# Twelve 1 MB loads of x issued as two transfers each, cut at partition 120, 104 or 88

## The chip, the cores and the metric

The kernel runs on one core of one Trainium2 chip. The metric is the device time of one execution in microseconds (us), taken as the median of repeated runs. The engines of the core are named as in the profile: PE (TensorE, matrix products and transposes), DVE (VectorE), ACT (ScalarE), POOL (GpSimd) and SP (SyncE, which here only issues DMA transfers). Sixteen DMA engines move data between the chip's memory (HBM) and the core's on-chip buffer of 128 partitions.

## The reference

A gated linear recurrence over 6336 time steps for 4 sequences of 256 channels, followed by a highway layer on every token:

```
sig = 1 / (1 + exp(-f_logit));  f = lower_bound + (1 - lower_bound) * sig
for t in range(S):                                   # S = 6336
    h = f[:, t] * h + (1 - f[:, t]) * x[:, t];  y[:, t] = h
H = max(y @ w_h, 0);  T = 1 / (1 + exp(-(y @ w_t + b_t)))
out = T * H + (1 - T) * y                            # 25344 tokens of 256 channels
```

Inputs x and f_logit and the output are 25.95 MB each in fp32, so at least 78 MB cross the memory interface.

## The kernel before

The tokens are cut into 29 **units** (lines 40 to 70). A large unit holds 1024 tokens as 128 partitions of 8 tokens, that is 8 KB of x per partition and 1 MB in all; there are 22 of them (units 3 to 13 and 15 to 25). The first three and the last three units are smaller, and unit 14 takes 192 tokens of each of the four sequences and moves them as four transfers of 32 partitions.

A unit goes through these steps; the letter is its name in the order:

- `l`, `x`: loads of f_logit and x, issued by SP (`load`, line 228). Tiles `l` and `x` have six buffers each.
- `u` (ACT): sigmoid of -f_logit. `b` (POOL, four of them as DVE): `bv` = u * x, a quarter of the unit at a time (line 252).
- `i`, `p` (PE): transposes of u and of bv, so that channels stand on partitions and tokens in a row. `f` (ACT): the gate.
- `s` (DVE): the recurrence as a scan along the tokens, one for each half of the channels (line 307). Each scan starts from the last column of the scan before it, so the units form one chain.
- `z`, `g` (PE): the two products of the highway layer; `t` (ACT), `d` (DVE), `E` on POOL and `e` on DVE: its gate and mix.
- `o` (PE): transposes back, with the sum; `c` (ACT): copy from the accumulator to `o` tiles (four buffers); `w` (SP): store, 512 KB each for the most part.

The order of the work on every engine is written out by hand in one string (lines 72 to 124); each token of it emits its instructions, and `pin` keeps them in that order. All transfers but two of 1 KB (`prm`, issued by ACT, two partitions each) are issued by SP, one after the other, in the order in which `l`, `x` and `w` stand in the string. SP waits in this order for what a transfer needs: a load of x for the last `bv` that read the buffer, a store for its copy, and each transfer also for the landing of the eighth transfer before it, since transfers take eight completion semaphores in turn. While SP waits, everything behind it in the string waits too.

`sides` (line 218) gives for a load the pairs of a tile's partitions and a part of the tensor in HBM. For a large unit that is one pair: 128 partitions, each reading 8 consecutive tokens.

Of the kernel before, what the change touches and what calls it, by code (L numbers as in the profile page):

```python
# [19 lines left out]
def kernel(  # L20
# [10 lines left out]
    nc = tc.nc  # L31
    B, S, D = x.shape
    assert (B, S, D) == (4, 6336, 256)
    P = 128
    NH = D // P
    NB = 8
# [3 lines left out]
    units = [  # L40
        (0, 128, 2, 0, 'y', 4, 0),
        (0, 128, 2, 256, 'y', 4, 0),
        (0, 128, 4, 512, 'y', 4, 0),
        (0, 128, 8, 1024, 'y', 4, 1280),
        (0, 128, 8, 2048, 'y', 4, 2048),
        (0, 128, 8, 3072, 'y', 4, 0),
        (0, 128, 8, 4096, 'y', 4, 2048),
        (0, 128, 8, 5120, 'yk', 4, 0),
# [82 lines left out]
    pin = tc.keep_in_program_order  # L131

    def sb(shape, dtype, name):
        return pool.tile(shape, dtype, tag=name, name=name, bufs=bufs.get(name, 1))
# [83 lines left out]
    def sides(n, t, full, j0, j1, stored=False):  # L218

        b, np_, nb, at = units[n][:4]  # L220
        if isinstance(b, int):
            return [(t[:np_, :j1 - j0], full[b, at + j0 * np_:at + j1 * np_, :].rearrange("(p j) d -> p j d", p=np_))]
        part = np_ // B
        return [(t[i * part:(i + 1) * part, :j1 - j0] if stored else t[i::B, :j1 - j0],
                 full[k, at[i]:at[i] + part * nb, :].rearrange("(p j) d -> p j d", p=part)[:, j0:j1])
                for i, k in enumerate(b)]

    def load(n, name, src):
        t = sb([P, NB, D], FP32, name)
        for dst, s in sides(n, t, src, 0, units[n][2]):  # L230
            pin(nc.sync.dma_start(dst, s))
        st[n][name] = t

    def do_l(n, k, eng, slot):
        load(n, "l", f_logit)

    def do_x(n, k, eng, slot):
        load(n, "x", x)
# [143 lines left out]
    for token in order.split():  # L382
        token, _, slot = token.partition(":")
        name = token.rstrip("v")
# [3 lines left out]
        n, _, k = name[1:].partition(".")  # L388
# [29 lines left out]
```

## Time and profile before

| | |
|---|---|
| time, median of 3 runs | 218.88 us (216.72, 218.88 and 220.64) |
| profiled execution, first to last instruction (span) | 215.2 us |
| the same execution's own time | not recorded beside its span |
| DMA traffic | 78.69 MB, mean 366 GB/s |
| read from HBM, written to HBM | 52.43 MB, 25.95 MB |
| transfers issued by SP | 125 |
| of these, loads of x of 1 MB | 22, median 13.8 us from issue to landing |
| granted TensorE clock, mean | 0.999 of full speed |

The profile is one execution. A line of a group or a timeline names the source line (L252 is line 252 above), the engine, the operation and the tiles that it writes and reads (`bv<-u,x`); "busy" is the time in which the engine worked. An idle stretch is put down to what ended it: `<-DMA x<-in_x_dram` means that a load of x landed and the waiting instruction went on. "SPq" is SP's queue of issues. Slices cut the span into 40 equal parts of 5.38 us. "Landing" is the time at which the last of a transfer's sixteen completions came in.

### The profile page before, as it was taken

The numbers are of one execution on the slowest core, as the hardware profiler recorded it, in microseconds if no ns is written. First come the engines' busy times: TensorE is split into PE (matmuls) and PEld (weight loads), VectorE is DVE, ScalarE is ACT, GpSimd is POOL, SyncE is SP. The second block draws the span as 40 slices with busy tenths as digits, with TensorE's granted clock in tenths as the row PEclk, the third lists the DMA queues.
The fourth block names the chain that finished last, engine by engine and source line by source line (L and its number), as shares of the span: only waits on it lengthen the run. The fifth ranks groups of instructions, "written<-read, shape, count | busy, mean of one in ns | idle before, by whom it ended". The sixth has DMA issues, their size and how long they took to land. (4 is left out here: it accounts for less than half of the span.)

```text
span 215.2 us, 4648 instructions
## 1 busy us (share of the span) xinstructions
PE 190.1 (88%) x1784; PEld 132.4 (62%) x1811; DVE 199.2 (93%) x164; ACT 195.9 (91%) x195; POOL 178.9 (83%) x166
## 2 busy tenths in 40 slices
PE   7477778988999799999998999999899999999881
PEld 3144456655766666675676766667676576776661
DVE  2789998999999899999998999999999999999960
ACT  4579889999999999999999999999999999999772
POOL 3045789997999999899998999887988999898910
PEclk9999999999999999999999999999999999999999
DMA  6999999999999999999999799998999999498275
GB/s 185 395 420 417 423 419 410 423 316 315 429 416 425 411 426 393 350 411 414 428 425 416 324 329 326 431 399 287 330 412 420 419 422 420 165 321 360 110 285 200
DMA packets 16750, 78.69 MB, mean 366 GB/s; under 512 B 2004, under 2 KB 2776, under 8 KB 11096
## 3 DMA queue, kind: packets, MB, share of 16 engines
q1 hardware_dynamic: 16720, 78.39, 92.7%
q8 instruction: 14, 0.23, 0.4%
q14 instruction: 8, 0.07, 0.1%
q10 hardware_dynamic: 8, 0.00, 0.0%
HBM read 52.43 MB, written 25.95 MB: 364 GB/s over the span
## 5 line engine op out<-in xcount | busy, mean ns | idle before, releaser
L252 POOL TENSOR_TENSOR bv<-u,x 128x512 bf16<-128x512 f16 x95 | 112.8, 1217 | 21.7 <-DVE w_sb L197 9.0
L307 DVE TENSOR_TENSOR_SCAN y<-f,y,bT 128x1024 bf16<-128x1024 f16 (+2 forms) x46 | 92.8, 2032 | 1.6 <-ACT f L276 0.9
L342 POOL TENSOR_TENSOR e<-d,t 128x512 bf16<-128x512 bf16 (+1 forms) x60 | 67.7, 1148 | 3.9 <-DVE e L342 3.0
L336 DVE SCALAR_TENSOR_TENSOR d<-y,ncc,g 128x1024 bf16<-128x1024 bf16 (+2 forms) x54 | 58.9, 1101 | 2.4 <-PE g L318 2.3
L331 ACT ACTIVATE t<-z,bt 128x1024 bf16<-128x1024 f32 (+3 forms) x58 | 57.9, 1019 | 2.0 <-PE z L318 1.3
L276 ACT ACTIVATE f<-uT,ncc 128x1024 f16<-128x1024 f16 (+3 forms) x53 | 55.4, 1057 | 4.2 <-PE uT L259 2.8
L318 PEld LDWEIGHTS <-w_sb 128*128 128x128 f16 x416 | 39.3, 99 | 32.2 <-issue 2.7
L372 ACT COPY o<-op 128x1024 f32<-128x1024 f32 (+2 forms) x53 | 51.2, 983 | 4.7 <-PE op L362 3.1
L243 ACT ACTIVATE u<-l 128x2048 f16<-128x2048 f32 (+3 forms) x29 | 49.2, 1695 | 3.8 <-DMA l<-in_f_logit_dram 3.6
L362 PE MATMUL op<-ident_b,e 128*128 128x128 bf16 x396 | 49.4, 219 | 1.0 <-DVE e L342 0.8
L318 PE MATMUL z<-y,w_sb 128*128 128x512 bf16 (+1 forms) x179 | 47.5, 372 | 1.2 <-DVE d L336 0.2
L318 PE MATMUL g<-y,w_sb 128*128 128x512 bf16 (+1 forms) x181 | 47.9, 372 | 0.7
L362 PEld LDWEIGHTS <-e 128*128 128x128 bf16 x396 | 44.0, 113 | 5.7 <-issue 2.2
L361 PE MATMUL op<-diag,y 128*128 128x128 f16 x368 | 45.9, 219 | 1.6 <-ACT o L372 0.9
L361 PEld LDWEIGHTS <-y 128*128 128x128 bf16 x368 | 41.0, 113 | 1.9
L290 PE MATMUL bT<-ident_f,bv 128*128 128x128 f32 x198 | 33.6, 283 | 7.2 <-POOL bv L252 2.5
L259 PE MATMUL uT<-ident_h,u 128*128 128x128 f16 x396 | 31.9, 221 | 7.7 <-DVE y L307 2.5
L259 PEld LDWEIGHTS <-u 128*128 128x128 f16 x396 | 26.6, 99 | 18.5 <-issue 7.9
L290 PEld LDWEIGHTS bT<-ident_f,bv 128*128 128x128 f32 x198 | 23.1, 142 | 17.0 <-POOL bv L252 3.8
L342 DVE TENSOR_TENSOR e<-d,t 128x512 bf16<-128x512 bf16 (+5 forms) x19 | 17.7, 943 | 1.0 <-PE op L362 0.7
L307 DVE TENSOR_TENSOR_SCAN y<-f,yr,bT 128x1024 bf16<-128x1024 f16 x4 | 9.3, 2333 | 0.0
L252 DVE TENSOR_TENSOR bv<-u,x 128x512 bf16<-128x512 f16 x4 | 3.4, 855 | 3.1 <-DMA x<-in_x_dram 3.1
(42 smaller groups left out, 48.9 us busy)
## 6 DMA issues: line engine op xcount, KB each, us to landing
out_dram<-o SPq DMA_DIRECT2D x46, 512.0 KB, 7.7
l<-in_f_logit_dram SPq DMA_DIRECT2D x22, 1024.0 KB, 11.1
x<-in_x_dram SPq DMA_DIRECT2D x22, 1024.0 KB, 13.8
l<-in_f_logit_dram SPq DMA_DIRECT2D x4, 256.0 KB, 8.7
x<-in_x_dram SPq DMA_DIRECT2D x4, 256.0 KB, 4.5
l<-in_f_logit_dram SPq DMA_DIRECT2D x2, 512.0 KB, 9.7
x<-in_x_dram SPq DMA_DIRECT2D x2, 512.0 KB, 7.5
out_dram<-o SPq DMA_DIRECT2D x3, 256.0 KB, 13.9
```

The source lines that it names most:

```text
L252: shared(pin(e.tensor_mul(st[n]["bv"][:np_, k].rearrange("p d j -> p j d"), st[n]["u"][:np_, q:q + 2], st[n]["x"][:np_, q:q + 2])), not eng)
L259: pin(nc.tensor.transpose(uT[:, j * np_:(j + 1) * np_], st[n]["u"][:np_, j, h * P:(h + 1) * P], ident_h[:np_, :np_]))
L276: pin(nc.scalar.activation(to, of, AF.Identity, scale=ncc[:, h:h + 1], bias=1.0))
L290: pin(nc.tensor.transpose(to, pair, ident_f[:np_, :np_]))
L307: pin(nc.vector.tensor_tensor_scan(y[:, c0:c0 + ln], st[n]["f", h][:, c0:c0 + ln], st[n]["bT", h][:, c0:c0 + ln], 0.0 if prev is None else ...
L318: pin(nc.tensor.matmul(p[:, a:e], w_sb[:, k, ki, m * P:(m + 1) * P], half(n, "y", ki)[:, a:e], start=ki == 0, stop=ki == NH - 1))
L331: pin(nc.scalar.activation(half(n, "t", m), st[n]["z", m][:, :tokens(n)], AF.Sigmoid, bias=bt[:, m:m + 1]))
L336: pin(nc.vector.scalar_tensor_tensor(half(n, "d", m), half(n, "y", m), ncc[:, m:m + 1], st[n]["g", m][:, :tokens(n)], op0=ALU.mult, op1=AL ...
L342: shared(pin(eng.tensor_mul(st[n]["e"][:, a:e], st[n]["d"][:, a:e], st[n]["t"][:, a:e])), eng is nc.gpsimd)
L361: pin(nc.tensor.matmul(o, half(n, "y", h)[:, cols], diag[:, h], start=True, stop=False))
L362: pin(nc.tensor.matmul(o, half(n, "e", h)[:, cols], ident_b, start=False, stop=True))
L372: pin(nc.scalar.copy(o[:np_, :w], st[n]["op", q][:np_, :w]))
```

## The change

`load` takes a cut for x in units with an odd number and the full eight tokens per partition. There the one transfer of 128 partitions becomes two, from partition 0 to the cut and from the cut to 128:

```diff
     def load(n, name, src):
         t = sb([P, NB, D], FP32, name)
+        cut = (120, 104, 88)[n % 3] if name == "x" and n % 2 and units[n][2] == NB else 0
         for dst, s in sides(n, t, src, 0, units[n][2]):
-            pin(nc.sync.dma_start(dst, s))
+            for p0, p1 in ((0, cut), (cut, P)) if cut else ((0, dst.shape[0]),):
+                pin(nc.sync.dma_start(dst[p0:p1], s[p0:p1]))
         st[n][name] = t
```

The condition holds for units 3, 5, 7, 9, 11, 13, 15, 17, 19, 21, 23 and 25. Units 3, 9, 15 and 21 are cut at 120 (120 + 8 partitions), units 7, 13, 19 and 25 at 104 (104 + 24), units 5, 11, 17 and 23 at 88 (88 + 40). SP then issues 137 transfers. The two parts stand next to each other in SP's order; both fill the same tile, and all other instructions keep their order on every engine.

## The prediction, made before the changed kernel was run

> **What bounds the kernel now.** I read the totals and the slices of the span first, then the DMA queues, then the waits, last the order of time on GpSimd and SyncE around the loads of x.
>
> The page's totals and slices (busy tenths, then GB/s, of 40 equal slices of 5.38 us):
>
> ```profile
> PE 190.1 (88%) x1784; PEld 132.4 (62%) x1811; DVE 199.2 (93%) x164; ACT 195.9 (91%) x195; POOL 178.9 (83%) x166
> ...
> DVE  2789998999999899999998999999999999999960
> ...
> DMA  6999999999999999999999799998999999498275
> GB/s 185 395 420 417 423 419 410 423 316 315 429 416 425 411 426 393 350 411 414 428 425 416 324 329 326 431 399 287 330 412 420 419 422 420 165 321 360 110 285 200
> ```
>
> Two things are full at once. VectorE has next to no idle time from 20 to 190 us, and the DMA engines run at a ceiling of about 420 GB/s except in short dips. So a load that comes late cannot be made up by a faster engine behind it.
>
> The DMA queue (packets, MB, share of 16 engines' span), then the issues of x:
>
> ```profile
> q1 hardware_dynamic: 16720, 78.39, 92.7%
> ...
> q10 hardware_dynamic: 8, 0.00, 0.0%
> ```
>
> The packets can be counted. Every partition row of a transfer is one packet: the 125 transfers of SP have 14720 rows, and 16720 - 14720 = 2000 = 125 x 16, so each posts sixteen completions, one per DMA engine. All of these have 32 or 128 partitions. Queue 10 holds the two loads of `prm`, two partitions each: 8 packets, that is two rows and two completions for each. **So a transfer of two partitions used two engines, one of 32 or 128 used all sixteen, always in equal shares.** A 1 MB load gives each engine 8 rows of 8 KB; such rows take 309 to 313 ns each in the trace's packet records, and loads standing back to back land every 2.50 us, which is 8 x 0.3125. An engine has this one rate; a load is there when its slowest engine is done.
>
> How late loads are, seen from GpSimd, which multiplies x by u (`bv`): its waits, and four of them in order of time (start, us, what, idle before and releaser):
>
> ```profile
> POOL bv L252 <- DMA x<-in_x_dram: 7.8, 6, 2.2
> ```
>
> ```profile
> 21.23 4.54 POOL L252 TENSOR_TENSOR bv<-u,x 128x512 bf16<-128x512 f16 x4 [2.19 <-DMA x<-in_x_dram]
> 27.77 4.54 POOL L252 TENSOR_TENSOR bv<-u,x 128x512 bf16<-128x512 f16 x4 [2.00 <-DMA x<-in_x_dram]
> ...
> 53.82 2.30 POOL L252 TENSOR_TENSOR bv<-u,x 128x512 bf16<-128x512 f16 x2 [1.52 <-DMA x<-in_x_dram]
> ...
> 163.40 1.18 POOL L252 TENSOR_TENSOR bv<-u,x 128x512 bf16<-128x512 f16 x1 [0.79 <-DMA x<-in_x_dram]
> ```
>
> These are units 4, 5, 9 and 23: their x landed at 21.07, 27.61, 53.66 and 163.27 by the semaphore records and was used 0.13 to 0.16 us later. Three of the four are loads that the change splits. The others come with 1 to 6 us in hand (x17: 116.29, used at 118.27).
>
> Last, SyncE, whose program order is the order of all transfers:
>
> ```profile
> 30.11 0.33 SPq L231 DMA_DIRECT2D l<-in_f_logit_dram  x1
> 44.96 0.34 SPq L379 DMA_DIRECT2D out_dram<-o  x1
> ...
> 116.60 0.42 SPq L231 DMA_DIRECT2D l<-in_f_logit_dram  x1
> 123.44 0.81 SPq L379 DMA_DIRECT2D out_dram<-o  x2
> ```
>
> Twice SyncE stands still before a store that waits for its copy, and the rings run dry. The sixteen completions of a load tell how far engines are apart: after such a pause all end within 0.3 us (126.20), in the middle of a stretch the last comes 2.0 to 2.9 us behind the first (x5: 24.73 to 27.61), because packets of instructions, 16 KB and about 1.0 us each, fourteen in all, take their turn on single engines.
>
> **The change, part by part.** Twelve loads, x3, x5 to x25 without the smaller units, become two transfers; the text that came with the change says ten, the program has twelve, four of each cut. No engine's order of work changes but SyncE's, which grows from 125 transfers to 137.
>
> *Twelve more issues and slots.* An issue occupies SyncE 0.33 to 0.45 us, 12 x 0.4 = 5 us on a queue that waits 103 us for copies: nothing. Each transfer waits for the eighth before it to land, so a pair takes two of eight places. Behind a wait there stand seven transfers, still some 3 MB or 7.5 us of work in the rings, against about 2.5 us from an issue to its first landing on an empty ring (44.96 to 47.66): nothing, and 2.5 us once if that cover failed.
>
> *A second wait in front of `bv`.* GpSimd waits for both halves. The median semaphore instruction at that line takes 42 ns: 12 x 0.04 = 0.5 us at most, some of it in waits that are there anyhow; I take 0.2.
>
> *Rows per engine.* This is the term that matters, and the trace has no transfer of 120, 104, 88, 40, 24 or 8 partitions. Bounds by counting rows: if the second half fell on those engines that the first had spared, the slowest engine still had 8 rows, nothing added. If shares are equal, as in every transfer that the trace has, and the engines are counted from the same end for both halves, 120 + 8 is 15 engines of 8 rows and 8 of 1; 104 + 24 is 13 of 8 and 12 of 2; 88 + 40 is 11 of 8 and 10 of 4. The first eight engines then carry 9, 10 and 12 rows where they had 8. That is 1 + 2 + 4 = 7 rows a triple, 28 in all: 28 x 0.3125 = 8.75 us. I take the second, since equal shares are what 2, 32 and 128 partitions show, and since the two 2-partition loads left just two engines behind (7.10 and 7.12 against 6.46 for the next, in the load issued at 2.11), not four: they chose the same two. [...]
>
> *How much of 8.75 us reaches the end.* The backlog grows load by load: 0.31 us at x3, 1.56 at x5, 2.19 at x7, 2.50 at x9, 3.75 at x11, 4.38, 4.69, 5.94 at x17, 6.56, 6.88, 8.13 at x23, 8.75 at x25. It is felt where a load has no margin: at x5 (1.6 us), at x9 (2.5), a little at x17 (5.9 against a margin of 2.0 plus the shift that GpSimd has by then), then at x23. After x23 no split load is tight (x25 has 4.6 us), and GpSimd and VectorE are full up to the end, so **the shift at x23 is about the shift of the end**.
> From above: if the slowest engine of before is one of the eight, it has no idle time at the pauses (it ended its loads at 124.93 and the stores behind them at 126.20, 1.27 us later, where 512 KB take 1.25), nothing is absorbed, and x23 comes 8.1 us late.
> From below: an ordinary engine idles about 1.1 us at the pause of 45 us (45.30 to 47.66, less 1.25 for the store), 2.5 us at that of 123 (122.18 to 125.90, less 1.25) and 0.3 at 146: 3.9 us of the backlog go there, and another 2.1 are hidden behind the engine that is last today; it also has its own share of the instruction packets, 14 x 1.0 / 16 = 0.9. So 8.1 - 3.9 - 2.1 + 0.9 = 3.0 us.
> Several engines are late by 0.7 to 2.8 us in each stretch, so one of the eight being among them is likelier than not; the middle, 5.5 us, is my value. Downstream of `bv` some 1.5 us of reserve lie before the scan (from the last `bv` to the scan 2.3 us at x5, where 0.6 at x3 was enough), but the chain that ends the span runs through GpSimd after 189 us, so I take nothing off for it.
>
> Sum: 5.5 + 0.2 = 5.7 us on the profiled span of 215.2, so 220.9. The median of the three runs stands 3.7 us above the span, its launch and end; with the same margin the time is **224.6 us**, by the bounds 221.9 to 227.2.
>
> **The rivals.**
> *Meeting on the way into the buffer memory (0.12).* With 15, 13 or 11 engines the rows may be dealt so that two engines write at the same place at once. [...] The nearest row for a 1 MB load that is slowed for whatever reason is x9, whose first completion stands 4.05 us behind that of the store before it, 1.55 more than usual. Twelve such are 18.6 us, nearly all on the full DMA rings: about 236. Against it: the stores of 32 neighbouring partitions, 128 KB each, completed 0.29 us apart (144.99 and 145.28), faster than any load.
> *Not slower: the late engines are the spared ones (0.13).* If the engines that trail today are those with the high numbers, the change takes 8 rows off them at a time; x5 would then land with the eight at 26.05 + 1.56 = 27.6 instead of 27.61, or, where the split puts a free engine under the next instruction packet, up to 1.3 us earlier, and x23 only by what is left. This decides if all laggards of a stretch stand above the eleventh engine; then the time is 217.6 to 220. For it: fourteen packets on single engines. Against: the engine that trails at x5 is one of the two that carried `prm`, the second value of that pair staying at 26.05.
> *Nothing happens (0.09).* Rows are spread evenly whatever the count, or the halves complement each other: 219. [...] The 2-partition loads, with two completions each, speak against an even spread.
>
> **How the numbers follow.** The backlog case has 0.66. A change of 2% (4.4 us) is about what a measurement of this kernel can tell from none, the three runs lying 1.8% apart. Of the 0.66 I put 0.57 above 223.3 us and 0.09 below; with the first rival slower has 0.69. The second rival gives 0.08 to within 2% and 0.05 to faster (1.3 us earlier makes no 2% without luck in the runs), the third all its 0.09 to within 2%: 0.26 and 0.05. The range reaches from 218 (the last rival, less half the spread of the runs) to 233 (the backlog in full with a third of the first rival), and leaves out most of that rival and the fastest corner of the second.
>
> **What would show it.** In the profile after: the first completion of an 88-partition half well before the last; x5, x9 and x23 landing 1.6, 2.5 and 3 to 8 us later; GpSimd's wait for x growing from 7.8 us to 12 or more; DMA's mean GB/s falling from 366 to about 356 with the same megabytes. It is wrong if rows of x take longer than 313 ns in number, if the sixteen completions lie no further apart than now, or if the loads land late and the end does not move.

## The result and the profile after

The changed kernel takes **260.12 us** (median of 4 runs, 255.8 to 264.77) against 217.84 us for the kernel before (4 runs, 216.72 to 220.64). Over the faster runs of each kernel (255.8 and 259.46 us of the changed one) the ratio is 1.182, 95% interval 1.173 to 1.190. The predicted way was right, the predicted size (224.6, at most 233) far too small.

The totals and slices of the changed kernel's page, as they were read for the kernel before (an execution of 260.79 us with a span of 259.0; its 40 slices are 6.48 us each):

```profile
PE 202.8 (78%) x1784; PEld 140.5 (54%) x1811; DVE 200.6 (77%) x164; ACT 198.2 (77%) x195; POOL 179.5 (69%) x166
...
DVE  3748894865898577999669898946999927899962
...
PEclk9675899997889979999889999977999998999998
DMA  7999999999989999699999999998899998939556
GB/s 222 379 221 413 228 306 229 201 332 340 310 360 228 374 380 263 227 351 238 408 424 393 262 395 318 242 359 248 309 352 285 312 412 283 380 143 356 234 209 228
DMA packets 16835, 78.69 MB, mean 304 GB/s; under 512 B 2088, under 2 KB 2860, under 8 KB 11180
...
q1 hardware_dynamic: 16804, 78.39, 92.4%
```

Every engine does the same work (VectorE 200.6 us after, 199.2 before); what grew is its idle time. The DMA engines are busy all the time, as before, and move the same 78.69 MB, but in many slices at 201 to 230 GB/s where they moved about 420. q1's share times the span was 0.927 x 215.2 = 199.5 us for each of the sixteen engines and is 0.924 x 259.0 = 239.3 us: 39.8 us more busy time for the same bytes, against 43.8 us more span. So the packets themselves became slow, which is most of the added time. The waits say who starves (engine, line and tile, what it waited for: us in total, times, longest):

```profile
POOL bv L254 <- DMA x<-in_x_dram: 36.1, 15, 5.3
ACT u L245 <- DMA l<-in_f_logit_dram: 22.2, 13, 4.4
...
ACT o L374 <- DMA out_dram<-o: 14.2, 11, 3.8
```

Not only x is late: loads of f_logit, which nobody touched, and stores are late too (3.6 and 0.4 us before). GpSimd's first multiplications of units 4, 5, 9 and 23 in order of time, the same four as before (line 252 has become line 254):

```profile
24.98 4.52 POOL L254 TENSOR_TENSOR bv<-u,x 128x512 bf16<-128x512 f16 x4 [2.05 <-DMA x<-in_x_dram]
35.81 4.53 POOL L254 TENSOR_TENSOR bv<-u,x 128x512 bf16<-128x512 f16 x4 [6.32 <-PE bT L292]
...
70.64 6.67 POOL L254 TENSOR_TENSOR bv<-u,x 128x512 bf16<-128x512 f16 x5 [4.18 <-DMA x<-in_x_dram]
...
204.15 1.16 POOL L254 TENSOR_TENSOR bv<-u,x 128x512 bf16<-128x512 f16 x1 [5.29 <-DMA x<-in_x_dram]
```

They start 3.8, 8.0, 16.8 and 40.8 us later than before (at unit 5 the profile names PE as the last releaser). Taken over all units the delay grows in steps, the largest at split loads: 4.0 us at unit 3, 4.3 more by unit 5, 5.1 more by unit 7, 5.4 at unit 17, 4.5 at unit 23, and 43.7 at the last unit.

The clearest view is a stretch around the first split load, before anything else differs. Both fences are windows of 4 us: the window, its length, then busy time and (instructions) of PE, PEld, DVE, ACT and POOL, the granted clock, the DMA share and GB/s. Before:

```profile
12.00:16.00 4.00, 2.91 (x23) 1.95 (x22) 3.33 (x5) 3.22 (x4) 1.55 (x2) 1.00 1.02 424
16.00:20.00 4.00, 2.67 (x23) 1.66 (x22) 4.00 (x7) 3.39 (x4) 2.79 (x2) 1.00 1.00 414
20.00:24.00 4.00, 3.28 (x29) 2.09 (x28) 4.00 (x3) 3.36 (x5) 2.77 (x3) 1.00 1.01 418
```

After:

```profile
12.00:16.00 4.00, 3.13 (x18) 1.99 (x15) 3.20 (x5) 1.72 (x4) 1.83 (x2) 0.65 1.04 240
16.00:20.00 4.00, 2.00 (x21) 1.81 (x22) 0.49 (x1) 3.03 (x4) 0.00 (x0) 0.78 1.01 238
20.00:24.00 4.00, 1.86 (x7) 0.81 (x6) 3.91 (x6) 2.76 (x2) 2.70 (x2) 0.50 1.00 416
```

The DMA share is 1.0 in both, the rate a little over half in two of three windows. The packet records show the same row by row: from 12.5 to 16 us, while the 120 partitions of x3 are loaded, an 8 KB row takes 500 to 670 ns (309 to 324 before); around 17 us, when the 8 partitions follow, up to 860; rows of the whole load behind it need until 19.5 us to come back to 313. In the whole run 2055 of the 5632 rows of 8 KB took more than 450 ns, and these had a median of 611, about twice 309; before, 252 rows took more than 450 ns.

The number of engines came out as the prediction had it. Short packets went from 2004 to 2088. By equal shares the three pairs post 15 + 8, 13 + 12 and 11 + 10 = 69 completions where three whole loads posted 48: 21 more, four times, is 84. For 120, 104, 88, 40, 24 and 8 partitions the shares were an estimate from the transfers of 2, 32 and 128; these 84 agree with it.

Both parts of a pair also fell on the same engines. The semaphore records name no engine, but they show it by time: of the sixteen completions of x6, the whole load of x behind the pair 88 + 40, five come at 31.58 to 35.99 us and eleven at 38.05 to 42.54. Eleven is the number of engines that the count gives to 88 partitions, and the other five ran ahead. First and last completion lie 11.0 us apart, for x8 13.1 us (48.69 and 61.77), where no load of x had more than 2.9 us before. So the unequal shares of the prediction are there, and larger in time than it had them, since the rows are slow.

### The profile page after: what moved, and what is told of

It reads as the page before. It is cut to its first block, busy times and chain, and to the rows that moved or that the text cites. A ratio compares the mean times of both kernels' runs of the same rounds, so it can differ in the third digit from the quotient of the medians.

```text
span 259.0 us, 4668 instructions
## 1 busy us (share of the span) xinstructions
PE 202.8 (78%) x1784; PEld 140.5 (54%) x1811; DVE 200.6 (77%) x164; ACT 198.2 (77%) x195; POOL 179.5 (69%) x166
## 2 busy tenths in 40 slices
DMA packets 16835, 78.69 MB, mean 304 GB/s; under 512 B 2088, under 2 KB 2860, under 8 KB 11180
## 4 chain that ended last, share of the span: by engine, by line
DMA 62%; PE 13%; ACT 6%; POOL 5%; issue 5%; SPq 4%; DVE 3%; POOLq 0%; ACTq 0%; DVEq 0%
DMA out_dram<-o 30%; DMA x<-in_x_dram 23%; DMA l<-in_f_logit_dram 9%; POOL e L344 3%; PE g L320 3%; SPq L233 3%; PE op L363 2%; PE z L320 2%; PE op L364 2%; ACT o L374 2%; PE bT L292 2%; PE uT L261 2%; DVE y L309 2%; POOL bv L254 2%; ACT t L333 2%
## 5 line engine op out<-in xcount | busy, mean ns | idle before, releaser
L338 DVE SCALAR_TENSOR_TENSOR d<-y,ncc,g 128x1024 bf16<-128x1024 bf16 (+2 forms) x54 | 59.4, 1107 | 16.8 <-PE g L320 15.8
L320 PEld LDWEIGHTS <-w_sb 128*128 128x128 f16 x416 | 41.3, 104 | 44.7 <-issue 18.3
L278 ACT ACTIVATE f<-uT,ncc 128x1024 f16<-128x1024 f16 (+3 forms) x53 | 54.3, 1031 | 6.8 <-PE uT L261 5.4
L320 PE MATMUL g<-y,w_sb 128*128 128x512 bf16 (+1 forms) x181 | 52.6, 403 | 7.2 <-ACT o L374 6.3
L363 PE MATMUL op<-diag,y 128*128 128x128 f16 x368 | 48.7, 226 | 11.0 <-ACT o L374 7.1
L364 PEld LDWEIGHTS <-e 128*128 128x128 bf16 x396 | 45.1, 116 | 16.0 <-issue 13.5
L320 PE MATMUL z<-y,w_sb 128*128 128x512 bf16 (+1 forms) x179 | 50.7, 392 | 3.2 <-ACT t L333 1.1
L364 PE MATMUL op<-ident_b,e 128*128 128x128 bf16 x396 | 52.2, 226 | 0.8 <-DVE e L344 0.8
L261 PEld LDWEIGHTS <-u 128*128 128x128 f16 x396 | 28.0, 102 | 31.1 <-issue 16.6
L292 PE MATMUL bT<-ident_f,bv 128*128 128x128 f32 x198 | 35.6, 297 | 7.7 <-POOL bv L254 2.9
L292 PEld LDWEIGHTS bT<-ident_f,bv 128*128 128x128 f32 x198 | 25.2, 152 | 16.9 <-POOL bv L254 6.8
```

Of the source, the lines that this page charges most:

```text
L261: pin(nc.tensor.transpose(uT[:, j * np_:(j + 1) * np_], st[n]["u"][:np_, j, h * P:(h + 1) * P], ident_h[:np_, :np_]))
L278: pin(nc.scalar.activation(to, of, AF.Identity, scale=ncc[:, h:h + 1], bias=1.0))
L292: pin(nc.tensor.transpose(to, pair, ident_f[:np_, :np_]))
L320: pin(nc.tensor.matmul(p[:, a:e], w_sb[:, k, ki, m * P:(m + 1) * P], half(n, "y", ki)[:, a:e], start=ki == 0, stop=ki == NH - 1))
L338: pin(nc.vector.scalar_tensor_tensor(half(n, "d", m), half(n, "y", m), ncc[:, m:m + 1], st[n]["g", m][:, :tokens(n)], op0=ALU.mult, op1=AL ...
L363: pin(nc.tensor.matmul(o, half(n, "y", h)[:, cols], diag[:, h], start=True, stop=False))
```

## The experiments

Four theories were set against each other. **Backlog**, the prediction's: the first engines of the count carry more rows at an unchanged 309 ns. **Places**: a pair takes two of the eight transfers that SyncE may have out (in the trace before, transfers take eight completion semaphores in turn). **Reads**: another order of addresses makes HBM slow. **Meeting**: engines write at the same part of the on-chip buffer at the same time, so that two share one way in; this is a conjecture, and what the runs can show of it is the rate. Except for the last, every kernel was run once. The kernel before, measured beside them, took 215.6 to 219.0 us, so a difference of 3 or 4 us between two single runs decides nothing; the differences on which the argument rests are 18 us and more.

**By tokens instead of partitions.**

```diff
-            pin(nc.sync.dma_start(dst, s))
+            cut = name == "x" and n % 2 and units[n][2] == NB
+            for j0, j1 in ((0, 4), (4, 8)) if cut else ((0, units[n][2]),):
+                pin(nc.sync.dma_start(dst[:, j0:j1], s[:, j0:j1]))
```

> The same twelve loads are split by tokens: two transfers of 128 partitions, four tokens (4 KB rows) each, so 137 transfers as in the changed kernel, sixteen engines and equal rows. Meeting theory (engines write at the same place of the buffer memory when a transfer's partitions are dealt out in another way than for 128): rows at 159 ns as for other 4 KB rows, 216 to 221 us. Backlog theory (28 more rows on the low engines): 216 to 221 us, no backlog. Slots theory (a pair takes two of the eight places behind which SP waits): as slow as the changed kernel, 250 us or more.

Measured 217.35 us (before 218.19). Twelve more transfers and places cost nothing that could be measured; the places theory ("slots" in the expectations) falls.

**Equal rows on all sixteen engines: 112 + 16 and 64 + 64.**

```diff
-        cut = (120, 104, 88)[n % 3] if ... else 0
+        cut = 112 if ... else 0      # the other kernel: 64
```

> The same twelve loads are cut at 112: 16 engines for both parts (16 completions each, 2200 short packets in all), 7 + 1 rows for every engine, so no backlog at all. Backlog theory: 216 to 221 us. Slots theory: 250 us or more. [...]

> The same twelve loads are cut in the middle: 64 + 64, 16 engines, 4 + 4 rows for every engine. Backlog theory: 216 to 221 us. Slots theory: 250 us or more. [...]

Measured 242.35 and 241.59 us, 24 and 23 us over the kernel before, without one row of backlog. For 64 + 64 the windows of the first split load:

```profile
12.00:16.00 4.00, 2.56 (x17) 1.64 (x15) 3.36 (x5) 1.68 (x3) 1.73 (x2) 1.00 1.07 227
16.00:20.00 4.00, 2.42 (x18) 2.02 (x19) 1.35 (x4) 3.02 (x4) 0.97 (x1) 0.57 0.98 342
```

The same slowness as in the changed kernel, where no engine has a row more than before. Backlog alone cannot do this.

**The reads kept, the partitions changed.** Four transfers of 32 rows read HBM in the same order in both kernels; they differ only in where the rows go.

```diff
-                pin(nc.sync.dma_start(dst, s))
+                for i in range(4):   # blocks
+                    pin(nc.sync.dma_start(dst[32 * i:32 * i + 32], s[32 * i:32 * i + 32]))
+                for i in range(4):   # the other kernel: every fourth partition
+                    pin(nc.sync.dma_start(dst[i::4], s[32 * i:32 * i + 32]))
```

> The same twelve loads become four transfers of 32 neighbouring partitions each (16 engines, 2 rows for each engine, so 8 rows in all and no backlog); the four read HBM in the order of addresses, 256 KB each. If engines meet at the on-chip buffer, because 32 or 64 neighbouring partitions have only half of its ways in: rows near 0.6 us, 235 to 250 us as with 64 + 64. If instead the order of reads in HBM makes rows slow: the same time as the kernel with every fourth partition. If only unequal rows matter: 216 to 222 us.

> As the kernel with four blocks of 32, the same four reads of HBM in the same order, but each fills every fourth partition of the tile (i, i + 4, ...), as the loads of unit 14 do in the kernel before; the rows of x thus stand in other partitions than the reference wants (tokens change places within a unit). Meeting at the buffer: rows at 309 to 320 ns as in unit 14, 216 to 222 us, some 20 us less than with blocks. Order of reads in HBM: no difference between the two, 235 us or more for both.

Measured 244.21 us with blocks, 219.95 us with every fourth partition. The windows of the blocks:

```profile
12.00:16.00 4.00, 2.81 (x16) 1.71 (x14) 2.98 (x5) 2.73 (x4) 1.00 (x1) 0.50 1.07 229
16.00:20.00 4.00, 3.00 (x22) 2.27 (x20) 0.94 (x2) 2.50 (x4) 0.90 (x1) 0.62 0.96 272
```

and of every fourth partition:

```profile
12.00:16.00 4.00, 3.84 (x19) 2.50 (x18) 3.14 (x6) 3.03 (x4) 2.29 (x2) 0.50 1.02 426
16.00:20.00 4.00, 2.62 (x25) 1.74 (x24) 4.00 (x6) 3.27 (x6) 2.82 (x2) 1.00 1.00 416
```

229 against 426 GB/s for the same reads, the same number of transfers, of engines and of rows. The order of reads is out here; the destination partitions decide.

**Two transfers, even and odd partitions.**

```diff
-                pin(nc.sync.dma_start(dst, s))
+                pin(nc.sync.dma_start(dst[0::2], s[0:64]))
+                pin(nc.sync.dma_start(dst[1::2], s[64:P]))
```

> As 64 + 64, the same two reads of HBM in the same order, but the first fills the even partitions and the second the odd ones (rows of x stand in other partitions than the reference wants). Both transfers thus reach all of the buffer. [...] Order of reads in HBM: 241 us as 64 + 64.

Measured 218.54 us against 217.24 before and 241.59 for 64 + 64 with the same reads. Its window of the first split load, at 418 GB/s where 64 + 64 had 227:

```profile
12.00:16.00 4.00, 2.79 (x21) 1.86 (x20) 3.35 (x5) 3.12 (x4) 1.75 (x2) 1.00 1.01 418
```

**A backlog by itself.** Behind every 1 MB load of x and l stands one transfer of 8 partitions, 4 KB each; the control moves 64 bytes.

```diff
+        if units[n][2] == NB:
+            i = at[0] % 4 + at[0] // 4 % 2 * 32
+            at[0] += 1
+            pin(nc.sync.dma_start(spare[i:i + 29:4, :1024], ...))   # control: :16
```

> The kernel before, with one small transfer more behind each 1 MB load of x and of l: 8 partitions (every fourth), 4 KB each, into a tile that nobody reads. These take 8 engines with one row of 159 ns each: 44 x 0.159 = 7.0 us more work on eight engines and none on the others, with no meeting. The prediction's backlog (8.75 us, of which 5.5 reach the end): 63% of 7.0 us, 4.4 us more than the kernel with the same transfers of 64 bytes. If a backlog is hidden: no difference between the two.

> The control to the 4 KB kernel: the same 44 transfers of 8 partitions, 64 bytes each, so no work for the engines to speak of, but 44 more of the eight places and 44 more issues. All theories: 217 to 222 us; what it stands above the kernel before is the price of places and issues.

Measured 219.51 us with 4 KB and 219.52 us with 64 bytes. The 44 transfers post 8 completions each (2352 in all), so the work did go to eight engines. On the way the lag can be seen: near 48 us the sixteen completions of a load of l end 3.2 us apart (45.18 to 48.42), in the control 2.4 us (45.37 to 47.74). At the end there is no sign of it, nor of the expected 4.4 us, though two single runs are weak evidence for so small a difference. Both kernels stand 3.9 us above the 215.6 us of the kernel before beside them, its fastest run on record; a small price of 44 more transfers is not excluded by single runs.

**Each cut for all twelve loads, and balanced cuts next to them.** The edit is the one number, as above.

> All twelve loads are cut at 120 (15 engines of 8 rows, then 8 of 1). Backlog theory: 12 rows of 0.31 us more, 3.75 us at the most, 218 to 222 us. Meeting theory: each pair costs about 3 to 3.7 us more as in the changed kernel, 250 to 265 us. Slots theory: 250 us or more.

> All twelve loads are cut at 104 (13 engines of 8 rows, 12 of 2; the low engines carry 10 rows). If meeting alone sets the time: about as the balanced cuts and 120 + 8, 240 to 248 us. If unequal rows add to it once rows are slow: above 120 + 8 and below 88 + 40, 250 to 262 us. By extra rows at 309 ns alone: 12 x 2 x 0.31 = 7.5 us, 218 to 226 us.

> All twelve loads are cut at 88 (11 engines of 8 rows, 10 of 4; the low engines carry 12 rows, the highest five none). Meeting alone: 240 to 250 us. Unequal rows added to slow rows: 262 to 285 us, so that the mean of the three cuts comes to the 260 us of the changed kernel, with DMA engines seen idle (fewer than 15 packets at work) in more of the time than with 120 + 8. Extra rows at 309 ns alone: 12 x 4 x 0.31 = 15 us, 220 to 234 us.

> All twelve loads are cut at 80 (sixteen engines, 5 + 3 rows for each). If unequal rows make 88 + 40 dearer: about as the other balanced cuts, 238 to 248 us. If the place of the cut does: near 88 + 40, 262 us or more.

> All twelve loads are cut at 96 (sixteen engines, 6 + 2 rows for each). If unequal rows make 104 + 24 dearer: 238 to 248 us. If the place of the cut does: near 104 + 24, 255 us or more.

Times, with the rows on the busiest engine as equal shares count them (an estimate; the records name no engine), the sum of all 8 KB rows' durations divided by sixteen engines (packet records) and the time in which 1 to 14 packets were at work, among 16 engines, after the first 10 us:

```
cut       rows on the busiest engine   us       8 KB rows, us   1 to 14 at work, us
none      8                            217      115.8           14.7
96 + 32   8                            234.8    135.3           11.0
112 + 16  8                            242.4    138.7           19.2
64 + 64   8                            241.6    139.5           14.3
80 + 48   8                            245.9    144.5           13.3
120 + 8   9                            247.1    143.9           16.4
104 + 24  10                           261.1    151.0           46.5
88 + 40   12                           271.1    154.6           59.2
changed   9, 10 and 12                 260.1    151.3           40.4
```

Two came out some 3 us below what was expected of them, 120 + 8 (250 us or more) and 96 + 32 (238 or more). The mean of the three cuts, 259.7 us, is the changed kernel. The balanced cuts beside 104 and 88 stand 26 and 25 us lower, so the place of the cut does not make these two dear, but the uneven split over 13 + 12 and 11 + 10 engines does. They pay twice: their rows are slower still (151.0 against 135.3 us, 154.6 against 144.5), and the three or five engines that have no row in the first part run dry (46.5 and 59.2 us against 11.0 and 13.3). The packet records show by how many: with 104 + 24 exactly 13 packets were at work for 22.5 us (0.8 with 96 + 32), with 88 + 40 exactly 11 for 21.8 us (0.9 with 80 + 48).

The table also tells how much of the added time the slow rows are. In the four balanced cuts the rows' sum grew by 19.5, 22.9, 23.7 and 28.7 us, and the time by 18, 25, 25 and 29: slow rows are all of it. With 104 + 24 and 88 + 40 they are 35.2 of 44 us and 38.8 of 54; of the 9 and 15 us that are left, 4.7 and 12.1 are idle time of the mean engine, while others still work off their rows.

**The same cut on stores.**

```diff
-            pin(nc.sync.dma_start(dst, src))
+            for p0, p1 in ((0, 64), (64, P)) if n % 2 and units[n][2] == NB else ((0, dst.shape[0]),):
+                pin(nc.sync.dma_start(dst[p0:p1], src[p0:p1]))
```

> The kernel before with the loads whole, but the 512 KB stores of the odd large units cut into 64 + 64 partitions (24 more transfers, 16 engines each). If meeting is a matter of writing into the buffer: rows of stores stay at 159 ns, 216 to 222 us. If reading from 64 neighbouring partitions is halved too, 24 stores of 1.25 us take 1.25 us more each: 235 to 248 us.

Measured 223.18 us against 217.24 before, between the two expected ranges. Most rows of stores stay at 159 ns; 529 of 6528 took over 250, against 154 before, and 3072 rows were in split stores. One run, and 5.9 us: reading the buffer seems to suffer, but far less than writing it.

**Even and odd partitions, each row in its place.**

```diff
-                pin(nc.sync.dma_start(dst, s))
+                for i, k in ((0, 2), (1, 2)) if ... else ((0, 1),):
+                    pin(nc.sync.dma_start(dst[i::k], s[i::k]))
```

> The twelve loads are split into even and odd partitions, each row of x in its right partition, so HBM is read in every second 8 KB row. Meeting at the buffer: free, as with the two halves of HBM in even and odd partitions (218.5 us), 215 to 221 us and within 2% of the kernel before. If that run was free only for its order of reads in HBM: 230 us or more.

Measured 217.03 us (10 runs, 215.35 to 217.93) against 216.98 (13 runs): a ratio of 0.9997, interval 0.9961 to 1.0034. On its page of the profile VectorE is full and the rates are back:

```profile
PE 190.8 (89%) x1811; PEld 132.3 (62%) x1811; DVE 199.2 (93%) x164; ACT 195.4 (91%) x195; POOL 178.3 (83%) x166
...
GB/s 220 383 426 422 416 420 414 423 357 353 393 419 424 414 424 368 356 396 419 429 416 416 348 339 343 419 386 284 347 416 419 419 419 416 182 319 367 102 306 191
```

So two transfers instead of one are free, if the cut is made across the partitions in this way. No kernel here is measurably faster than the kernel before.

## Why the prediction went wrong

*What bounds the kernel:* right. VectorE and DMA were both full, and time lost on the rings came out at the end nearly whole: 39.8 us more busy time of the DMA engines, 43.8 us more span.

*Issues, places, second wait:* right. The split by tokens, with the same 137 transfers, took 217.35 us against 218.19. The 3.7 us from the span to the time were too many: every run with both on record stands 1.7 to 1.9 us above its span, and the rest was spread between runs. Beside 43.8 us this does not matter.

*Rows per engine:* the counting was right (84 more completions; that both parts are counted from the same end was an estimate, which the completions of x6, five and eleven, fit), but the step that failed stands behind it: **the 28 rows were priced at 0.3125 us, and the other rows of the split loads at no change, since "an engine has this one rate".** It does not: in the split loads rows took 500 to 670 ns, and rows of the transfers behind them were slow too, for some 2 us behind the first pair. The durations of all 8 KB rows, divided by sixteen engines, grew from 115.8 to 151.3 us: the term was 35.5 us on the mean engine, and no run shows the 8.75 us on eight. The prediction's own sign of being wrong, rows of x above 313 ns in number, is what the trace shows. What decides the rate is into which partitions a transfer writes; the pairs of kernels with the same reads show this for 32 partitions (244.21 against 219.95 us, 229 against 426 GB/s in the first window) and for 64 (241.59 against 218.54, 227 against 418). That two engines then share one way in was not shown: no record names the engines or the ways. For the cuts of the change itself (120, 104 and 88) the cause is carried over from those pairs. That the time rose, as forecast, is in part luck: the balanced cuts, with no backlog at all, cost 18 to 29 us.

*How much of it reaches the end:* that 5.5 of 8.75 us, 63%, reach the end was not borne out for rows at full rate: none of 7.0 us was seen there, in single runs. That the margins and the pauses hide it is the likely reason, not a shown one. Where rows are slow it is not hidden: the unequal cuts of 104 and 88 stand 25 us above their balanced neighbours. There the lag is of another size, 11 and 13 us between the first and the last completion of x6 and x8 in the changed kernel, and part of the engines run dry. A kernel with unequal rows as large as these and no slow rows was not tried, so the two effects are not separated fully.

*The rivals.* The first, meeting on the way into the buffer, comes nearest to what was found, with a chance of 0.12 and a price of 236 us that was too low: 1.55 us for a pair, taken from x9, where 43.7 / 12 = 3.6 us were paid. Its condition, 15, 13 or 11 engines, was too narrow: cuts with sixteen engines and equal rows are slow as well. The row that spoke against it was misread: the stores of 32 neighbouring partitions *read* the buffer, and the split of the stores shows that reading suffers far less (5.9 us for 64 + 64, where the loads cost 23). The row that would have helped is unit 14's loads, which write every fourth partition at full rate (6 KB rows in 234 ns, as 8 KB in 312): it shows that 32 partitions can be fast if they are spread. The second and third rival, at 217.6 to 220 us, fell with the time itself. The third took an even spread, or halves that complement each other, for harmless; 64 + 64, with 4 + 4 rows on every engine by the count, cost 23 us.

Why 120 + 8 is dear no run shows: its first part fills all but eight partitions, and its rows still took 500 to 670 ns in the changed kernel.

## What to carry to other kernels

Where a transfer writes in the buffer can set its rate: 229 GB/s into blocks of 32 partitions, 426 into every fourth. In this kernel, with the rings full, each of the seven cuts tried between partition 64 and 120 cost 18 to 54 us in twelve loads, while cuts by the free dimension or into even and odd partitions cost nothing that could be measured. Price a changed transfer by a row with the same shape and the same direction, and when the trace has none, let the upper bound be a rate divided by two, as here, for all of its bytes and for some behind it, not a few rows more. Count completions (packets of 4 bytes) to learn how many engines a transfer used (the 84 more here are what 15 + 8, 13 + 12 and 11 + 10 make), and look how far apart they come to learn whether the engines are evenly loaded.

## What the runs showed that was not expected

A disturbed load slows whole loads behind it: after the first pair rows came back to 313 ns only some 2 us later, at 19.5 us. And the granted clock of TensorE was lower in the kernels where it idled more: 0.999 in the profile before with PE busy for 88% of the span, 0.917 in the changed kernel's with 78%, 0.93 to 0.97 in the other slow ones (0.97 to 1.0 in the kernel before beside them); matmuls of `g` took 403 ns on the mean against 372. It does not cause the slow loads: the kernel with every fourth partition shows 0.50 in its first window above, at 426 GB/s, and `PEclk` of the changed kernel is low in slices of either rate (0.6, 0.7 and 0.5 in the second to fourth, at 379, 221 and 413 GB/s).
